# GpSimd's first zeroes moved ahead, the second weight block and four loads moved behind the first bias, eight zero groups for nine

## The chip, the cores and the metric

The kernel runs on one core of one Trainium2 chip. The metric is the device time of one execution in microseconds (us). Engines: TensorE (PE; its weight loads are PEld), VectorE (DVE), ScalarE (ACT), GpSimd (POOL), and SyncE (SP), whose queue issues most DMA transfers; ACT's queue issues a few.

## The reference

Attention over 4 batches of 8 heads (576 positions, 64 wide) with a causal mask and a forgetting bias, then two feed-forward layers on the 2304 x 512 result:

```python
scores = scale * np.matmul(q, k.transpose(0, 1, 3, 2))
cum = np.cumsum(np.maximum(s, 0.0), axis=-1)
bias = -(cum[:, :, :, None] - cum[:, :, None, :])
scores = np.where(causal, -1000000000.0, scores + np.minimum(bias, 0.0))
attn = softmax(scores)                    # with 1e-9 added to the sum
x = (attn @ v), heads side by side        # 2304 x 512
h = x @ w_in                              # 512 -> 2048
g = np.where(h >= 1, h, np.where(h <= -1, 0.0, (h + 1) ** 2 / 4))
x = g @ w_out                             # 2048 -> 512
out = ((x @ w_a) * (x @ w_b)) @ w_out2    # 512 -> 1536 -> 512
```

The weights arrive as 64-bit floats and are turned into 32-bit ones on the chip.

## The kernel before

The program is written as a list of some thousands of operations, each with the engine it runs on, an estimate of its time, a key (an intended moment) and the tiles that it reads and writes. A planner (`Plan.run`) walks through them on a simulated clock and takes on each engine the ready operation with the lowest key. So the order of the instructions on every engine comes from the keys, the estimates (`lat` for a transfer, the number in braces for an engine) and the earliest moments (`at`) in the code. A changed estimate can reorder instructions far from the place where it stands.

How work is staged: for each head, PE multiplies q by k for five blocks of up to 116 query rows (L731 for the first eight heads, which carry the bias as four more rows of q and k; L740 later, in split precision), DVE masks each block and takes its least value (L759, called "least"), ACT takes the exponential (L774), PE transposes it with an identity (L801), ACT or DVE copies the transposed block out (L397, L399), and for a pair of heads PE multiplies by v (L831). L865 spreads the inverse sums of a pair of heads for the first batch. In between the 64-bit weights are converted block by block: `wlow` and `wabs` on ACT (L978, L980), then four operations on DVE (`wclamp` L982, `wshift` L984, `wsign` L986, `wadd` L988), a cast to the high half on ACT or GpSimd (`whi`, L397 or L401) and the low half on DVE (`wlo`, L1004). From about 95 us on the two feed-forward layers run (L1034, L1245).

The first 15 us, which the change touches: PE multiplies zeros in groups of four 128x512 matmuls (L582, `WARM` groups). Tile `gate` takes the four parts of s and, in its second half, their running sum (`cums`, L650 to L657, on DVE). GpSimd builds `ones` (L587, L589), the mask `hide` (L632, L633), the identity, and zeroes part of the two `qk_tiles` (L601), which serve the split heads from the ninth head on. The bias rows of a head are DMAs out of `gate` into the head's raw tile `qkraw` (or `ysf`, for the third and fourth head), the ones rows are DMAs out of `ones`; both must land before the head's first score matmul. Two weight blocks fit in the staging tile `cvf`.

The function `fill`, called where the planner sees PE idle for over 0.5 us, issues matmuls on the zero tile `still` (L1471) if the idle stretch starts after a given moment of the planner's clock (`if lo < 8: return`). DMA queues run in order: an issue that waits holds up those behind it on the same engine.

Of the kernel before, what the change touches and what calls it, by code (L numbers as in the profile page):

```python
# [58 lines left out]
PAIRS = 2  # L59
WARM = 9  # L60
FILL = 0.5
# [253 lines left out]
def tile_forgetting_attention_two_ffn(  # L315
# [246 lines left out]
    for t in range(NG):  # L562
        dma(
            START + 2,
            lambda t=t: gate.t[t * BH : (t + 1) * BH, 0],
            lambda: s,
            BH * S * 4,
            (),
            [(gate, ("s", t))],
            "s",  # L570
            q=(SP, ACT)[t % 2],
        )
    s_parts = [(gate, ("s", t)) for t in range(NG)]
# [24 lines left out]

    op({POOL: 2.5}, START + 2, build_ones, (), [(ones, 0)], name="ones")
    for n in range(2):  # L600
        op({POOL: 1.6}, START + 6 + n, lambda e, n=n: nc.gpsimd.memset(f32(qk_tiles[n][:D, 2:4]), 0.0), (),  # L601
           [("q_zero", n)], name="zero")
# [62 lines left out]
    op({DVE: 0.4}, START + 2, cums(0), (), [(gate, "cum")], name="cum0")  # L665
    op({DVE: 3.9}, START + 3, cums(1), s_parts, [(gate, "cum")], name="cum1")
    op({ACT: 0.7}, later + 4, cums(2), [(gate, "cum")], ["terms0"], name="terms0", at=later - 5.0)
# [8 lines left out]
    def load_head(b, h, key):  # L676
# [5 lines left out]
        if b * H + h < QK32:  # L682
            st["qk"] = raw
            for w in range(2):
                dma(key, lambda w=w: raw.t[:D, w], lambda w=w: qk[bh, :, w], D * S * 4, (), [(raw, (0, w))], "qk", issue=0.6,
                    at=0.0 if bh < 2 else 8.4)
            first = bh == 0
            dma(START + 3 if first else key, lambda: raw.t[D : D + NG, 1], lambda: gate.t[:, 1].rearrange("(t h) n -> h t n", h=BH)[bh],
                NG * S * 4, [(gate, "cum")], [(raw, "bias")], "bias", issue=0.56)
            load_v(b, h, st, key)  # L690
# [21 lines left out]
    def load_v(b, h, st, key):  # L712
        vr = st["v"] = Ref(v_room, key)
        dma(key + 0.5, lambda: vr.t, lambda: v[b * H + h], P * NQ * D * 4, (), [(vr, 0)], "v", at=8.4)

# [233 lines left out]
    def convert(name, f, key):  # L949
# [3 lines left out]
        if paired:  # L953
            src = w[:, 2 * P * f : 2 * P * (f + 1)].rearrange("(c p) f -> p c f", p=P)
            soon = name == "in" and f == 0
            dma(START + 2.3 + 0.1 * f if soon else key - LEAD, lambda: wide.t.rearrange("p (c n) -> p c n", c=NC), lambda: src, P * 4096, (),
                [(wide, 0)], "wide", q=ACT if soon else SP, lat=WIDE_LAT)
        else:
# [504 lines left out]
    def fill(lo, hi, o, places):  # L1463
        taken = {n for r, where, _ in places if r.room is banks for n in where}
        if lo < 8:
            return
# [50 lines left out]
```

## Time and profile before

| | |
|---|---|
| device time, three runs | 1034.84, 1040.04, 1040.10 us; median 1040.04 |
| the profiled execution: device time | 1048.49 us |
| its span, first to last instruction | 1046.8 us |
| TensorE's granted clock, mean over the span | 0.986 of full |
| busy: PE, DVE, ACT, GpSimd | 98%, 79%, 56%, 9% |

The profiled execution took 8.45 us more than the median of the runs, and 1.69 us of its time lie outside the span. A granted clock of 1.00 is the upper of TensorE's two levels (2.4 GHz), 0.50 the lower (1.2 GHz). Busy shares are means over the whole span; the first 60 us and the rest have different limits.

### The profile page before, as it was taken

To read this page: it belongs to the slowest core of one execution; us is meant where nothing else is said; L and a number is where in the kernel's file an instruction comes from. 1 tells how busy PE (TensorE), PEld (TensorE's weight loads), DVE (VectorE), ACT (ScalarE), POOL (GpSimd) and SP (SyncE) were. 2 spreads that over 40 slices of the span, in tenths; PEclk is the share of its full clock that TensorE was granted. 3 is DMA by queue.
4 is the path that set the end of the run, shared out by engine and by line. 5 is a ranking of instruction groups with operands and counts; after the bars stand their busy time and mean duration, and the time that the engine had idled before them with its cause. 6 is when DMAs were issued, how large, how long until landed. Compare 5 with 4: busy or idle time off the path is not lost.

```text
span 1046.8 us, 18557 instructions
## 1 busy us (share of the span) xinstructions
PE 1029.4 (98%) x6829; PEld 960.8 (92%) x6829; DVE 824.5 (79%) x1594; ACT 584.7 (56%) x1233; POOL 93.0 (9%) x125
## 2 busy tenths in 40 slices
PE   8999999999999999999999999999999999999998
PEld 4668879998888999999999999999999999999998
DVE  6699988549899999997989798586984658872765
ACT  4688887568578775576474754443443324433330
POOL 2133222103222110000000000000000000000000
PEclk7799999999999999999999999999999999999999
DMA  7476678847767679568273575546554433472501
GB/s 206 133 205 196 199 215 278 251 161 245 238 222 241 205 261 313 201 223 266 81 267 106 170 254 195 184 170 229 210 202 153 171 131 134 173 256 92 182 1 61
DMA packets 89916, 201.00 MB, mean 192 GB/s; under 512 B 9697, under 2 KB 40673, under 8 KB 89057
## 3 DMA queue, kind: packets, MB, share of 16 engines
q1 hardware_dynamic: 89168, 199.11, 57.0%
q8 instruction: 54, 0.88, 0.3%
q10 hardware_dynamic: 656, 0.71, 0.2%
q14 instruction: 38, 0.30, 0.1%
HBM read 146.96 MB, written 52.22 MB: 190 GB/s over the span
## 4 chain that ended last, share of the span: by engine, by line
PE 77%; DVE 12%; ACT 4%; DMA 3%; issue 3%; POOL 1%; SPq 0%; DVEq 0%; POOLq 0%; ACTq 0%
PE pp L1034 29%; PE pp L1245 18%; PE ps L1245 13%; PE ps L1034 5%; PE ps L831 4%; PE ps L801 3%; PE ps L740 2%; DVE p L759 1%; PE ps L731 1%; DMA cvf<-in_w_in 1%; DVE ysf L1343 1%; PE pp L740 1%; DVE cvf L986 1%; DVE cvf L988 1%; DVE g L1080 1%
## 5 line engine op out<-in xcount | busy, mean ns | idle before, releaser
L1034 PE MATMUL pp<-g,whl 128*128 128x288 f32 (+1 forms) x1920 | 296.0, 309 | 2.3 <-DVE xcf L1277 1.1
L1034 PEld LDWEIGHTS pp<-g,whl 128*128 128x128 f32 x1920 | 281.9, 188 | 5.9 <-DVE xcf L1277 1.6
L1245 PE MATMUL pp<-form,xbt 128*128 128x384 f32 (+1 forms) x480 | 88.3, 321 | 0.4 <-DVE xbt L1134 0.4
L774 ACT ACTIVATE p<-p,mx 116x464 f32<-116x464 f32 (+4 forms) x140 | 81.8, 587 | 10.8 <-DVE mx L759 10.3
L1245 PE MATMUL pp<-form,xat 128*128 128x384 f32 (+1 forms) x480 | 87.6, 321 | 0.0
L1034 PE MATMUL ps<-g,whl 128*128 128x384 f32 (+1 forms) x480 | 81.0, 317 | 0.0
L1245 PEld LDWEIGHTS pp<-form,xbt 128*128 128x128 f32 x480 | 77.5, 188 | 1.1 <-DVE xbt L1134 0.6
L1245 PEld LDWEIGHTS pp<-form,xat 128*128 128x128 f32 x480 | 77.3, 188 | 0.9 <-DVE esf L1264 0.9
L1343 DVE TENSOR_TENSOR ysf<-pp,ysf 128x576 f32<-128x576 f32 (+1 forms) x62 | 51.1, 826 | 32.8 <-PE pp L1034 32.7
L1034 PEld LDWEIGHTS ps<-g,whl 128*128 128x128 f32 x480 | 75.9, 188 | 0.1
L397 ACT COPY pt<-ps 112x112 f32<-112x112 f32 (+4 forms) x175 | 64.7, 398 | 12.9 <-PE ps L801 12.1
L1245 PE MATMUL ps<-form,xbt 128*128 128x384 f32 (+1 forms) x360 | 66.3, 320 | 0.0
L1245 PE MATMUL ps<-form,xat 128*128 128x384 f32 (+1 forms) x360 | 65.8, 321 | 0.0
L801 PE MATMUL ps<-ident,p 116*116 116x116 f32 (+2 forms) x420 | 63.9, 271 | 1.7 <-ACT pt L397 0.7
L759 DVE CUSTOM_DVE_ANT_0 p<-ps,hide 116x116 f32<-116x116 f32 (+1 forms) x112 | 49.0, 451 | 18.8 <-PE ps L740 11.9
L978 ACT ACTIVATE cvf<-cvf 128x512 uint32<-128x512 uint32 x68 | 46.3, 680 | 26.8 <-DVE cvf L988 21.5
L1245 PE MATMUL pp<-form,cvt 128*128 128x384 f32 x288 | 58.0, 338 | 0.9 <-DVE form L1211 0.4
L1245 PEld LDWEIGHTS ps<-form,xbt 128*128 128x128 f32 x360 | 58.3, 188 | 0.2 <-DVE esf L1264 0.2
L1245 PEld LDWEIGHTS ps<-form,xat 128*128 128x128 f32 x360 | 58.0, 188 | 0.1
L801 PEld LDWEIGHTS ps<-ident,p 116*116 116x116 f32 (+2 forms) x420 | 46.8, 138 | 12.3 <-ACT pt L397 4.0
L831 PE MATMUL ps<-pt,v 116*64 116x344 f32 (+4 forms) x448 | 56.0, 391 | 0.0
L1129 DVE TENSOR_TENSOR sums<-sums 128x256 f32<-128x256 f32 x128 | 54.2, 424 | 2.1
(165 smaller groups left out, 1923.4 us busy)
## 6 DMA issues: line engine op xcount, KB each, us to landing
whl<-keep_out SPq DMA_DIRECT2D x60, 512.0 KB
qkraw<-in_qk SPq DMA_DIRECT2D x104, 144.0 KB
cvf<-in_w_out SPq DMA_DIRECT2D x28, 512.0 KB
keep_out<-whl SPq DMA_DIRECT2D x28, 512.0 KB
sums<-keep_b SPq DMA_DIRECT2D x36, 256.0 KB
keep_in<-whl SPq DMA_DIRECT2D x16, 512.0 KB
cvf<-in_w_in SPq DMA_DIRECT2D x15, 512.0 KB
cvf<-in_w_a SPq DMA_DIRECT2D x12, 512.0 KB
```

Source lines behind the costliest of these rows:

```text
L397: nc.scalar.copy(o, i)
L731: nc.tensor.matmul(pv()[:r, a, :w], t.t[: D + NG, 0, QT * i : n], t.t[: D + NG, 1, a * w : (a + 1) * w], start=True, stop=True,)
L740: nc.tensor.matmul(pv()[:r, a, :w], t.t[:, 2 * u, QT * i : n], t.t[:, 2 * u + 1, a * w : (a + 1) * w], start=(u == 0), stop=(u == 1),)
L759: nc.vector.tensor_tensor_reduce(out=psl(pref.t)[:r].rearrange("q (g n) -> q g n", g=parts), in0=pv()[:r, :parts, :w], in1=hide[:r, lag : ...
L774: nc.scalar.activation(p, p, AF.Exp, bias=mx.t[:r], scale=-1.0, accum_out=sm.t[:r, h % 2, i : i + 1])
L801: nc.tensor.transpose(pt.t[: rows[j], (j - j0) * QT : (j - j0) * QT + r], psl(pref.t)[:r, QT * j : QT * j + rows[j]], ident[:r, :r],)
L831: nc.tensor.matmul(ps.t[n * D : (n + 1) * D, q0 - lo : hi - lo], st["v"].t[: rows[j], j], st["pt"][g].t[: rows[j], REG_AT[g][j] + q0 - lo ...
L978: op({ACT: act(512) + 0.07}, k, lambda e: nc.scalar.activation(up(), low(), AF.Copy, scale=2.0**-29), [(wide, 0)], [(we, 0)], name="wlow")
L1034: nc.tensor.matmul(bank_of(ps, a)[:, :w1], w(wu), x(xu)[:, a * w1 : (a + 1) * w1], start=(k == 0 and t == 0), stop=(k == len(terms) - 1 an ...
L1129: return lambda e: nc.vector.tensor_tensor(one(o), one(x), one(y), op=how)
L1245: nc.tensor.matmul(at(to), by_pair(st.t)[:, at_w, wu, g], forms[b, layer, g].t[:, x, xu], start=fresh and k == 0, stop=k == len(terms) - 1 ...
L1343: nc.vector.tensor_tensor(o, i, o, op=ALU.add)
```

## The change

It moves GpSimd's two zeroings of `qk_tiles` ahead of `ones` (keys START+1, with an estimate of 1.0 for 1.6), issues one zero group less, lets `fill` act only from 14 us of the planner's clock, gives the second weight block an earliest moment of 9.5, v one of 9.0 for 8.4 and the q and k of the third and later heads 9.6 for 8.4, and changes four estimates (s transfers 2.6 for 2.0, the first bias transfer 1.2 for 2.0, `cums` 3.4 for 3.9, `ones` 2.2 for 2.5).

```diff
-WARM = 9
+WARM = 8
...
             q=(SP, ACT)[t % 2],
+            lat=2.6,
...
-    op({POOL: 2.5}, START + 2, build_ones, (), [(ones, 0)], name="ones")
+    op({POOL: 2.2}, START + 2, build_ones, (), [(ones, 0)], name="ones")
     for n in range(2):
-        op({POOL: 1.6}, START + 6 + n, lambda e, n=n: nc.gpsimd.memset(f32(qk_tiles[n][:D, 2:4]), 0.0), (),
+        op({POOL: 1.0}, START + 1 + 0.1 * n, lambda e, n=n: nc.gpsimd.memset(f32(qk_tiles[n][:D, 2:4]), 0.0), (),
            [("q_zero", n)], name="zero")
...
-    op({DVE: 3.9}, START + 3, cums(1), s_parts, [(gate, "cum")], name="cum1")
+    op({DVE: 3.4}, START + 3, cums(1), s_parts, [(gate, "cum")], name="cum1")
...
-                    at=0.0 if bh < 2 else 8.4)
+                    at=0.0 if bh < 2 else 9.6)
...
-                NG * S * 4, [(gate, "cum")], [(raw, "bias")], "bias", issue=0.56)
+                NG * S * 4, [(gate, "cum")], [(raw, "bias")], "bias", issue=0.56, lat=1.2 if first else 2.0)
...
-        dma(key + 0.5, lambda: vr.t, lambda: v[b * H + h], P * NQ * D * 4, (), [(vr, 0)], "v", at=8.4)
+        dma(key + 0.5, lambda: vr.t, lambda: v[b * H + h], P * NQ * D * 4, (), [(vr, 0)], "v", at=9.0)
...
-                [(wide, 0)], "wide", q=ACT if soon else SP, lat=WIDE_LAT)
+                [(wide, 0)], "wide", q=ACT if soon else SP, lat=WIDE_LAT,
+                at=9.5 if name == "in" and f else 0.0)
...
-        if lo < 8:
+        if lo < 14:
             return
```

On SP's queue at the start of the program (`cvf<-in_w_in` is a weight block, `qkraw<-in_qk` q and k of a head, `qkraw<-g` its bias, `ysf` the third and fourth head). Before:

```order
L409 DMA qkraw_75<-in_qk 64x576 x2
L409 DMA cvf<-in_w_in 128x4x256
L409 DMA qkraw_74<-g_199 4x576
L409 DMA v_282<-in_v 128x320
L409 DMA qkraw_75<-g_199 4x576
...
L409 DMA ysf<-g_199 4x576
L409 DMA cvf<-in_w_in 128x4x256
L409 DMA qkraw_74<-in_qk 64x576 x2
```

and of the change, the same place:

```order
L409 DMA qkraw_75<-in_qk 64x576 x2
L409 DMA qkraw_74<-g_200 4x576
L409 DMA v_281<-in_v 128x320
L409 DMA qkraw_75<-g_200 4x576
...
L409 DMA ysf<-g_200 4x576
L409 DMA qkraw_74<-in_qk 64x576 x2
L409 DMA qkraw_74<-g_200 4x576
L409 DMA cvf<-in_w_in 128x4x256 x2
```

The first bias now stands directly behind the first two heads' q and k; the second weight block moved from ahead of it to behind the fifth head's q, k and bias, where it goes out together with the third.

On DVE, from the last operation of the running sum to the second "least" of the first head. Before:

```order
L657 TENSOR_SCALAR g_199<-g_199,mids 128x576
L982 TENSOR_SCALAR cvf<-cvf 128x512
...
L988 ISA cvf<-cvf 128x1024
L982 TENSOR_SCALAR cvf<-cvf 128x512
L984 TENSOR_SCALAR cvf<-cvf 128x512
L759 ISA p_0_299,mx_0_300<-ps_82,hide 116x116
L759 ISA mx_0_300 116x1
L759 ISA p_0_309,mx_0_310<-ps_83,hide 116x232
```

and of the change (lines from L573 on stand one to two further down):

```order
L658 TENSOR_SCALAR g_200<-g_200,mids_72 128x576
L984 TENSOR_SCALAR cvf_211<-cvf_211 128x512
...
L990 ISA cvf_211<-cvf_211 128x1024
L1006 TENSOR_TENSOR whl0_285<-cvf_211,whl0_285 128x2x256
L760 ISA p0_0_290,mx0_0_291<-ps0_82,hide_70 116x116
L760 ISA mx0_0_291 116x1
L760 ISA p1_0_294,mx1_0_295<-ps1_83,hide_70 116x232
```

Two operations on the second weight block no longer stand ahead of the first "least"; the low half of the first block stands there in their place. Its high half is cast on ACT now, which GpSimd did before.

On GpSimd, the start of the program. Before:

```order
L587 MEMSET g_202 4x576
L589 ISA
L589 AFFINE_SELECT g_202<-g_202 4x576 x2
...
L601 MEMSET qk_77 64x1152
L601 MEMSET qk_78 64x1152
L912 MEMSET sm_268 116x10
```

and of the change:

```order
L602 MEMSET qk_77 64x1152
L602 MEMSET qk_78 64x1152
L588 MEMSET g_217 4x576
L590 ISA
L590 AFFINE_SELECT g_217<-g_217 4x576 x2
L633 MEMSET hide 116x580
```

The two zeroings moved from the end of GpSimd's first stretch to its beginning; the instructions themselves are the same.

## Rows read from the trace of the kernel before

**Rows 1.** The page: span; PE's granted clock in 40 slices, tenths.

```profile
span 1046.8 us, 18557 instructions
...
PEclk7799999999999999999999999999999999999999
```

**Rows 2.** Windows, PE: start:end, length, busy (x), clock, DMA share, GB/s.

```profile
11.29:12.76 1.47, 0.01 (x2) 1.00 0.84 260
12.76:14.17 1.41, 1.40 (x6) 1.00 0.72 217
14.17:14.61 0.44, 0.00 (x0) 0.56 0.49 75
14.61:37.70 23.09, 23.09 (x77) 0.50 0.50 155
37.70:41.50 3.80, 3.80 (x15) 0.50 0.08 33
```

**Rows 3.** Timeline of DVE, 0 to 15 us: start, length, instruction.

```profile
4.25 2.28 DVE L652 TENSOR_SCALAR g<-g 128x576 f32<-128x576 f32 x1 [2.30 <-DMA g<-in_s]
...
8.60 0.52 DVE L657 TENSOR_SCALAR g<-g,mids 128x576 f32<-128x576 f32 x1
9.10 0.43 DVE L982 TENSOR_SCALAR cvf<-cvf 128x512 f32<-128x512 f32 x1
...
10.74 0.69 DVE L988 CUSTOM_DVE_ANT_0 cvf<-cvf 128x1024 uint16<-128x1024 uint16 x1
13.48 0.43 DVE L982 TENSOR_SCALAR cvf<-cvf 128x512 f32<-128x512 f32 x1 [2.04 <-ACT cvf L980]
...
14.28 0.27 DVE L759 CUSTOM_DVE_ANT_0 p<-ps,hide 116x116 f32<-116x116 f32 x1
```

**Rows 4.** Timeline of GpSimd, 0 to 7 us.

```profile
4.16 2.05 POOL L601 MEMSET qk<- 64x1152 f32 x2
```

**Rows 5.** Timeline of ACT and of its queue (ACTq), 0 to 15 us.

```profile
2.86 2.07 ACTq L409 DMA_DIRECT2D qkraw<-g  x2
4.96 1.28 ACT L978 ACT_TABLE_LOAD   x1 [4.96 <-issue]
7.83 0.67 ACT L978 ACTIVATE cvf<-cvf 128x512 uint32<-128x512 uint32 x1 [1.59 <-DMA cvf<-in_w_in]
```

**Rows 6.** Timeline of SP's queue, 0 to 15 us.

```profile
8.07 0.41 SPq L409 DMA_DIRECT2D cvf<-in_w_in  x1
9.15 0.62 SPq L409 DMA_DIRECT2D qkraw<-g  x1
```

**Rows 7.** Chain that ended last, 0 to 16 us: start, length, what.

```profile
8.07 4.68 DMA cvf<-in_w_in
...
14.61 1.89 PE ps L731 x2
```

**Rows 8.** Windows: PE, PEld, DVE, ACT, GpSimd busy, clock, DMA share, GB/s.

```profile
14.61:41.50 26.89, 26.89 (x89) 17.66 (x91) 15.90 (x46) 13.49 (x40) 2.06 (x4) 0.50 0.44 138
...
42.10:57.30 15.20, 15.08 (x99) 10.50 (x98) 14.05 (x40) 12.83 (x38) 3.33 (x5) 1.00 0.68 215
...
42.10:95.50 53.40, 52.02 (x359) 38.42 (x358) 50.29 (x138) 45.82 (x131) 16.91 (x22) 1.00 0.69 210
```

**Rows 9.** Groups by line, DVE, 42.1 to 96 us: busy us, mean ns.

```profile
L399 DVE COPY pt<-ps 116x232 f32<-116x232 f32 (+5 forms) x11 | 4.5, 415 | 0.9 <-ACT g L774 0.5 <-PE ps L801 0.2
L988 DVE CUSTOM_DVE_ANT_0 cvf<-cvf 128x1024 uint16<-128x1024 uint16 x6 | 4.1, 686 | 0.0
L1004 DVE TENSOR_TENSOR whl<-cvf,whl 128x512 fp32r<-128x512 f32 x6 | 4.1, 682 | 0.0
```

**Rows 10.** Tile whl on ACT: ns least/median/most, first and last start.

```profile
L397 ACT CAST whl<-cvf x13: 608/622/627, 153.2 to 579.4; 128x512 fp32r<-128x512 f32 x13
```

**Rows 11.** Timeline of PE: the zero groups, and the first pair's product with v.

```profile
1.26 9.27 PE L582 MATMUL ps<-esf 128*128 128x512 bf16 x36 [1.26 <-DVE esf L576]
...
37.69 4.42 PE L831 MATMUL ps<-pt,v 116*64 116x344 f32 x20
```

## Prediction

> **What bounds the kernel now.** I read the page first. The span is 1046.8 us, and the granted clock stands at its upper level in every slice but the first two [rows 1]. So only the first 50 us look unlike the rest. I then cut them into windows of PE: after the zero matmuls and the filler PE idles 1.47 us, runs the first six score matmuls in 1.41 us, idles 0.44 us, and in that second pause the clock falls to its lower level [rows 2]. It stays there from 14.61 to 41.50 us with PE busy all the time. It comes back inside the first pair's twenty matmuls with v, which begin at 37.69 [rows 2, 11]. In this stretch DVE is busy 15.90 of 26.89 us and ACT 13.49 [rows 8]: PE at the lower clock sets the pace. From 42 us to the first feed-forward step, about 95 us, DVE is busy 50.29 of 53.40 us beside a PE at 52.02 [rows 8]; both are near their limit there.
>
> Last I read the chain of waits up to 15 us. It runs through the second weight block (4.68 us from issue to landing), ACT's and DVE's work on that block, the first "least" (L759), and from 14.61 on the second batch of score matmuls, which needs the bank that "least" empties [rows 7]. DVE's timeline shows why: its queue is in order, its work on the first block ends at 11.43 (10.74 + 0.69), then it waits for the second block, and the first "least" starts only at 14.28 [rows 3].
>
> **The change part by part.** *Second weight block behind the bias.* It takes two DVE operations out from ahead of the first "least", and the wait for the block with them. What stands there now is the low half of the first block, which waits for the high half, now on ACT. Worked out: DVE ends the first block at 11.43 as before [rows 3]; the cast on ACT takes 0.62 us by the row of later casts there [rows 10], so 12.05, with the hand-overs about 12.1; the low half takes 0.68 [rows 9], so 12.8. "Least" starts at 12.8 to 12.9 for 14.28: 1.4 us earlier.
>
> Is anything else late then? The bias must have landed. SP issued it at 9.15, behind the block [rows 6]; PE could start at 12.76 [rows 2], at most 3.6 us after the issue. With no block ahead it lands no later than that. Even at 12.76 the first of the three score blocks is through by about 13.1, and the gain is 1.2. Lower bound of the gain on this path 1.0, upper 1.4; I take 1.3, since both ends lie close.
>
> *Zeroes first.* VectorE's first operation on s took 2.28 us at 4.25, while one on the same tile with the same shape took 0.52 [rows 3]; the zeroing ran on GpSimd from 4.16 to 6.21 [rows 4], and the slow operation ended 0.3 us behind it. Moved, the zeroes run from about 0.8 on, when DVE waits for s anyway. At 4.25 GpSimd is then still at `ones` or the mask, in shorter instructions. So the stall shrinks by 0 to 1.76 us. This brings the running sum and the bias forward, but "least" hangs on the weight block (12.8), not on the bias, so I cost it at nothing. If that cover went, at most 1.76 us would show. `ones` is ready 2.05 us later, near 4.9 for 2.86. ACT issues its two transfers then. Before, the two took 2.07 us and the table load 1.28 [rows 5]; so ACT is free between 7.4 (two plain issues of some 0.6 each) and 8.3, and it needed the weights only at 7.83 [rows 5]. That costs 0 to 0.45 us, and is the 1.0 above.
>
> *One zero group less, and no filler.* Both run while PE has nothing else to do; they free no time. The zeroes end a microsecond sooner, near 9.5 (1.26 + 9.27 x 32/36) [rows 11], and no filler follows. If the bias lands between 10 and 11.5, PE again has a pause before the six score matmuls and a second one, 11.4 to 12.9 or so, behind them. Before, pauses of 1.47 and 0.44 us were followed by the lower clock [rows 2]; pauses at least as long should bring it too. The order has the same work up to the first pair's matmuls with v, so I carry over 23.09 + 3.80 us at the lower clock unchanged, begun 1.3 us earlier.
>
> *Blocks converted later.* By the order, between the first pair's scaling (42 us) and the first feed-forward step DVE gets three more copies of transposed blocks, two more low halves and one addition less than before: 3 x 0.415 + 2 x 0.682 - 0.686 = 1.9 us [rows 9]. Idle DVE time there is 3.11 us [rows 8]. So this costs between nothing, if it goes into those gaps, and 1.9 us; I take 0.5, nearer to nothing, since ACT has fewer copies in return. The later estimates and moments (v, q and k of later heads, transfers of s) only change when the planner wants them; SP's order shows v behind its head's bias as before, and I cost them at nothing: v is first read behind all of a pair's scores. From about a fifth of PE's order on, the two programs have the same sequence; what PE gains before is kept to the end.
>
> Sum: -1.3 + 0.5 = -0.8 us on a profiled execution of 1048.49 us, so 1047.7. That execution is 8.45 us above the median of the three runs; on the median, 1040.04 - 0.8 = **1039.2 us**. With the bounds the terms alone reach from -1.8 (nothing lost on DVE, and the 1.4, with some of the stall) to +0.9 (1.0 gained, 1.9 lost): 1038 to 1041. The clock makes the wide range. Three runs of one program lie 5 us apart, and the profiled one 8 above them; the stretch at the lower clock is the one place that I see which could differ so much between executions.
>
> **Rivals.** *The clock stays up, or returns early.* Against it stands that less PE work covers the first 13 us than before, and that 26.89 us of full PE work did not lift it [rows 8]. For it speaks that PE goes from zeroes to scores with a shorter first pause if the bias lands by 10, and that a run at 1034.84 exists. Price: the stretch of 26.89 us would be bound by DVE's 15.90 [rows 8], 11 us less; the second pair of heads, at the upper clock, took 15.20 [rows 8], which agrees. 1039.2 - 10 = 1029; if it returns half-way, 1034.
>
> The Trainium skill's page TensorE: Matmul & The Clock Gate (Part 1) says that the lower rate is the idle state and that sustained activity releases it. By that rule the clock should return soon after 14.61, since PE is never idle, and the time would be near the 1034 of the half-way case or below it. The trace disagrees: 0.50 for 26.89 us at a PE shown busy throughout [rows 8]. I go by the rows.
>
> *The clock returns one pair later: slower.* The place is the first pair's matmuls with v. The clock rose 3.8 us after their start, with 0.6 us of them left [rows 2, 11]. If it does not rise within them, the next such run of twenty is a pair later, and that pair's 15.20 us [rows 8] become about as long as the first pair's 27.5 (14.61 to 42.10): +12, so 1051. It decides between the cases whether those twenty matmuls are just long enough; that the work begins 1.3 us earlier could tip it.
>
> *DVE or weights late.* The third to fifth weight blocks stand two to nine places later on SP's queue. If one is late for its feed-forward step, PE waits a conversion (five DVE operations, some 3 us): 1042; two such, 1045.
>
> *Nothing comes of it.* ACT's cast, now ahead of the first "least", comes 1.4 us late, behind ACT's own transfers: 1040, no change.
>
> **Chances.** Half a per cent, 5.2 us, is about what a measurement tells from no change: below 1034.8 is faster, above 1045.2 slower. My forecast with the small rivals (DVE, weights, nothing) has 0.57, all of it within that. The clock up or early: 0.27, nearly all faster. A pair later: 0.11; weights late twice or more: 0.05; both slower. So faster 0.27, same 0.57, slower 0.16. For 8 in 10 the range takes in all of the middle, the clock up at 1029, and the late weights; part of the pair-later case stays out: 1029 to 1047. The likeliest case alone: 1037 to 1042.
>
> **What would show it.** Right: DVE's first operation on s well under 2.28 us; the second weight block issued after 15 us; the first "least" at 12.8 to 13.3; the clock at its lower level from about 13 to 40 us, rising in the first pair's matmuls with v; those starting near 36.4; the same PE order and idle time from 160 us on. Wrong: a clock that stays at the upper level through 15 to 40 us, or is still at the lower one at 45; or PE waiting for weights between 60 and 160 us by more than the trace of before shows.

## The result: the change is half a per cent slower

| | before | changed |
|---|---|---|
| median of 20 executions | 1039.13 us | 1045.22 us |
| least and most | 1034.73, 1051.27 | 1037.14, 1051.39 |
| the profiled execution, its span | 1048.49, 1046.8 | 1050.23, 1048.4 |
| mean granted clock of the profiled execution | 0.986 | 0.988 |

The ratio of changed to before is 1.0056, with a 95% interval from 1.0032 to 1.008. The forecast was 1039.2 us and no change that can be told; the time lies inside the stated range of 1029 to 1047 and 6 us above the forecast.

The twenty times of the changed kernel fall into groups by their mean granted clock: 7 executions at 0.999 or 1.0 took 1037.14 to 1040.12 us (median 1039.17), 4 at 0.993 took 1042.89 to 1045.54, and 9 at 0.988 to 0.991 took 1045.75 to 1051.39. Of the kernel before, 148 executions with a listed clock lie beside the experiments below, e1's twelve among them (two more, and one each of e14 and e16, took 1090 us and more; they were disturbed and are left out of every count): 54 at 0.999 or more (median 1035.72), 74 at 0.996 to 0.998 (median 1039.18), and only 20 at 0.993 or less (median 1048.9). So both profiled executions, before and changed, are of the low-clock kind. That kind is 13 of 20 for the changed kernel and 20 of 148 for the one before.

The page of the changed kernel, span and PE's clock in 40 slices; it answers to [rows 1] and looks nearly as before:

```profile
span 1048.4 us, 18534 instructions
...
PEclk8799999999999999999999999999999999999999
```

Windows of PE, answering to [rows 2] and [rows 8] (start:end, length, busy, clock, DMA share, GB/s):

```profile
10.60:12.04 1.44, 1.41 (x6) 1.00 0.32 76
12.04:14.40 2.36, 0.00 (x2) 1.00 0.74 215
14.40:16.00 1.60, 1.60 (x6) 0.97 0.69 213
16.00:38.00 22.00, 22.00 (x79) 0.50 0.35 100
38.00:40.00 2.00, 2.00 (x10) 0.55 0.79 253
40.00:42.00 2.00, 2.00 (x17) 1.00 0.29 81
```

The first six score matmuls now run at 10.6 us, and behind them PE stands still for 2.36 us in one piece. Before there were two pauses, 1.47 and 0.44 us, with those six matmuls between them. The clock falls near 15.9 and is back near 39.9: 24.0 us of a fully busy PE at the lower level, for 27 before.

The timeline of the changed kernel, all engines, 0 to 15 us, answering to [rows 3] to [rows 6] and [rows 11]:

```profile
0.80 2.04 POOL L602 MEMSET qk<- 64x1152 f32 x2 [0.29 <-POOLq L1512]
1.26 9.24 PE L583 MATMUL ps<-esf 128*128 128x512 bf16 x32 [1.26 <-DVE esf L577]
...
4.06 0.46 DVE L653 TENSOR_SCALAR g<-g 128x576 f32<-128x576 f32 x1 [2.11 <-DMA g<-in_s]
...
5.07 1.82 ACTq L409 DMA_DIRECT2D qkraw<-g  x2
...
7.49 0.62 SPq L409 DMA_DIRECT2D qkraw<-g  x1
...
9.16 0.68 ACT L980 ACTIVATE cvf<-cvf 128x512 uint32<-128x512 uint32 x1 [0.96 <-DMA cvf<-in_w_in]
...
12.08 0.69 DVE L990 CUSTOM_DVE_ANT_0 cvf<-cvf 128x1024 uint16<-128x1024 uint16 x1
...
12.81 0.62 ACT L397 CAST whl<-cvf 128x512 fp32r<-128x512 f32 x1 [2.41 <-DVE cvf L990]
...
13.46 0.69 DVE L1006 TENSOR_TENSOR whl<-cvf,whl 128x512 fp32r<-128x512 f32 x1 [0.68 <-ACT whl L397]
14.06 0.27 DVE L760 CUSTOM_DVE_ANT_0 p<-ps,hide 116x116 f32<-116x116 f32 x1
...
14.40 1.03 PE L732 MATMUL ps<-qkraw 68*116 68x464 f32 x2 [2.36 <-DVE mx L760]
```

The reader is to see three things. VectorE's first operation on s takes 0.46 us for 2.28, and the first bias leaves SP at 7.49 for 9.15: the front of the change works. The first weight block reaches ACT at 9.16 for 7.83, although its issue did not move; the table load was through at 8.2 (6.92 + 1.28), so it is the transfer that came late. And DVE stands at 12.77 with "least" next in need but the low half next in order: the low half waits 0.68 us for ACT's cast, runs 0.69, and "least" comes at 14.06, 0.22 us earlier than before.

The chain of the changed kernel up to 15 us, answering to [rows 7]:

```profile
1.74 7.40 DMA cvf<-in_w_in
...
12.81 0.62 ACT whl L397
13.43 0.03 issue
13.46 0.04 DVE whl L1006
13.49 0.57 issue
14.06 0.27 DVE p L760
...
14.40 1.03 PE ps L732 x2
```

It now runs through the first block for the second, and then through the cast and the low half.

Where did the time between the two profiled executions go? PE of the changed one is about 2 us ahead at 40 to 90 us, has lost that by 320 us, and loses another 1.7 us near 611 us, where ACT waits 2.4 us for transfers whose eight issues took SP's queue 4.96 us for 3.64 in the same order. That last is a chance of the execution: in e3's profile, of the same order, ACT waits 0.7 us there. The pair therefore doesn't explain the 6 us of the medians. The count of low-clock executions does, and it needed many executions to be seen: the changed kernel's seven high ones have a median of 1039.17 us, next to the 1039.13 of before's twenty.

One gain is hidden in this. None of the changed kernel's 20 executions lies at 0.996 to 0.998, where half of those of before lie (74 of 148). That group comes from a stall near 64 us, shown under e1 and e13, and the order of the change doesn't have it (e3, below).

### The profile page after: what moved, and what is told of

Same layout as the page of the kernel before. It is cut to its first block, busy times and chain, and to the rows that moved or that the text cites. A ratio compares the mean times of both kernels' runs of the same rounds, so it can differ in the third digit from the quotient of the medians.

```text
span 1048.4 us, 18534 instructions
## 1 busy us (share of the span) xinstructions
PE 1027.3 (98%) x6818; PEld 959.3 (91%) x6818; DVE 822.9 (78%) x1597; ACT 588.6 (56%) x1237; POOL 87.3 (8%) x118
## 4 chain that ended last, share of the span: by engine, by line
PE 75%; DVE 14%; DMA 3%; ACT 3%; issue 3%; POOL 1%; SPq 1%; ACTq 0%; DVEq 0%; POOLq 0%
PE pp L1036 28%; PE pp L1247 18%; PE ps L1247 13%; PE ps L1036 5%; PE ps L832 4%; PE ps L802 2%; DVE p L760 2%; PE ps L741 1%; PE ps L732 1%; DVE cvf L988 1%; DVE cvf L990 1%; DVE qk L708 1%; DVE g L1082 1%; DMA qkraw<-in_qk 1%; DVE whl L1006 1%
## 5 line engine op out<-in xcount | busy, mean ns | idle before, releaser
L397 ACT COPY pt<-ps 116x348 f32<-116x348 f32 (+5 forms) x172 | 63.0, 393 | 12.3 <-PE ps L802 11.6
L980 ACT ACTIVATE cvf<-cvf 128x512 uint32<-128x512 uint32 x68 | 46.2, 679 | 30.2 <-DVE cvf L990 24.9
L802 PEld LDWEIGHTS ps<-ident,p 116*116 116x116 f32 (+2 forms) x420 | 47.0, 138 | 13.2 <-ACT pt L397 4.0
```

Source lines behind the costliest of these rows:

```text
L397: nc.scalar.copy(o, i)
L802: nc.tensor.transpose(pt.t[: rows[j], (j - j0) * QT : (j - j0) * QT + r], psl(pref.t)[:r, QT * j : QT * j + rows[j]], ident[:r, :r],)
L980: op({ACT: act(512) + 0.07}, k, lambda e: nc.scalar.activation(up(), low(), AF.Copy, scale=2.0**-29), [(wide, 0)], [(we, 0)], name="wlow")
```

## The experiments

Each kernel was timed beside the one before on the same chip, in four groups (e1 to e4, e5 to e8, e9 to e12, e13 to e16), each on a chip of its own; ratios are against the kernel before of the same group. Its low share was 7 of 35, 2 of 35, 3 of 33 and 8 of 33 in these groups, so small differences in count mean little, and medians of different groups are compared only roughly. The median is that of all executions; "high" counts executions with a mean clock of 0.999 or more and gives their median, "low" those at 0.993 or less.

| run | median us | ratio, 95% interval | high | low | of |
|---|---|---|---|---|---|
| e1, before again | 1038.75 | 0.9987 (0.9957 to 1.0016) | 2, 1036.07 | 0 | 12 |
| e2, before, fewer zeroes | 1041.24 | 0.9997 (0.9955 to 1.004) | 3, 1035.29 | 5 | 12 |
| e3, changed, pause filled | 1037.62 | 0.9961 (0.9924 to 0.9997) | 12, 1037.62 | 0 | 12 |
| e4, before, pauses filled | 1038.19 | 0.9973 (0.9941 to 1.0006) | 5, 1035.92 | 0 | 12 |
| e5, changed, longer zeroes | 1038.86 | 1.0021 (0.9988 to 1.0054) | 7, 1037.83 | 4 | 12 |
| e6, changed without zeroes first | 1038.35 | 1.0009 (0.9985 to 1.0033) | 9, 1038.17 | 3 | 12 |
| e7, before, block late | 1040.70 | 1.0034 (1.0012 to 1.0057) | 7, 1039.88 | 1 | 12 |
| e8, changed without block late | 1046.61 | 1.0079 (1.0047 to 1.0112) | 5, 1040.48 | 6 | 12 |
| e9, changed, two neighbours swapped | 1038.20 | 1.0013 (0.9991 to 1.0036) | 8, 1037.76 | 3 | 12 |
| e10, changed, zeroes moved back | 1044.52 | 1.0047 (1.0013 to 1.0082) | 5, 1037.19 | 7 | 12 |
| e11, e4 with more filler | 1037.67 | 0.9998 (0.9987 to 1.001) | 11, 1037.67 | 0 | 11 |
| e12, changed, table load early | 1045.90 | 1.006 (1.0026 to 1.0095) | 4, 1038.24 | 5 | 9 |
| e13, e4 with one block earlier | 1035.64 | 0.9972 (0.9948 to 0.9995) | 11, 1035.57 | 0 | 12 |
| e14, before, zeroes first alone | 1039.92 | 1.002 (0.9992 to 1.0048) | 6, 1038.76 | 3 | 11 |
| e15, before, estimates alone | 1042.93 | 1.0038 (1.0 to 1.0075) | 5, 1040.15 | 3 | 12 |
| e16, before, eight groups alone | 1038.41 | 0.9979 (0.9949 to 1.0009) | 6, 1035.09 | 4 | 11 |

Two theories stood at the start: that the change loses the clock in the opening, by the pause behind the first six scores, and that its re-planned order makes PE wait later on. The rivals on the first were that less zero work alone loses it, and that something ahead of the low half comes late (the zeroings in one piece, or the table load). The expectations name them by letters.

The zeroes and the filler never reach the output; the other edits change only the order or the moments of work that is there anyway, but for e12's, whose small result is overwritten.

**e1, the kernel before once more.** No edit.

> The kernel before, unchanged, for the granted clock of each of its executions. Theory A (opening clock: the change makes TensorE's clock fall to its lower level more often or for longer in the first 40 us): most executions here show a mean granted clock of 0.995 or more, against 7 of 20 of the changed kernel; those at 1.00 take 1035 to 1037 us and the few at 0.988 take 1048 or more. Theory B (schedule: the re-planned order costs some us between 42 and 200 us whatever the clock does): the clocks are spread as in the changed kernel, and at equal clock this kernel is 3 to 6 us faster.

Measured: no execution with a low opening, and a profile of the common kind, at 1039.31 us. Its windows of PE:

```profile
16.00:38.00 22.00, 21.91 (x143) 1.00 0.80 241
...
63.00:66.00 3.00, 0.69 (x5) 1.00 1.04 227
66.00:68.00 2.00, 2.00 (x17) 0.81 0.94 380
68.00:70.00 2.00, 2.00 (x13) 0.50 0.10 39
```

The stretch from 16 to 38 us that ran at 0.50 in [rows 8] runs at 1.00. In the opening, the pauses of [rows 2] are missing too: PE runs its first eight score matmuls on end, though the second block still stands ahead of "least" on DVE.

```profile
12.03 2.39 PE L731 MATMUL ps<-qkraw 68*116 68x116 f32 x8
```

In place of the low opening a short dip follows a stall of PE near 64 us. The waits of PE from 58 to 68 us name ACT, and the waits of ACT the fifth block of the first feed-forward weight (`PE ps L801 <- ACT pt L397` and `ACT cvf L980 <- DMA cvf<-in_w_in`, 2.3 and 2.4 us, once each); the chain that ended last says the same:

```profile
57.35 7.42 DMA cvf<-in_w_in
...
64.85 0.18 ACT cvf L980
...
65.41 0.26 ACT pt L397
...
65.71 0.41 PE ps L801 x2
```

So the profiled execution of before was not the typical one.

**e2, fewer zeroes in the order of before.** The ninth group issues nothing, the filler acts from 14 us; no other instruction moves.

```diff
-               nc.tensor.matmul(idle.t, warm[:, :P], warm, start=True, stop=True) for _ in range(4)
...
+               nc.tensor.matmul(idle.t, warm[:, :P], warm, start=True, stop=True) for _ in range(4 if n < 8 else 0)
...
-        if lo < 8:
+        if lo < 14:
```

> The kernel before with only the four matmuls of the last zero group and the seven filler matmuls near 10 us left out; every other instruction and its order as before. Theory A: the longer pause ahead of the first scores (some 3.2 us for 1.5) brings the lower clock oftener: median 1042 to 1047, half of the executions at a mean clock under 0.994. Theory B: 1038 to 1040, as before.

Measured: a median 2.5 us above e1's, just under the 1042 to 1047 that theory A expected, and 5 of 12 executions at the low clock, for 7 of 35 of the kernel before in the same group. The ratio can't be told from 1. In its profile PE pauses 1.93 us ahead of the scores and the clock is low from about 13.2 to 30.2 us. Less zero work alone may make the low opening more common; twelve executions don't show it.

**e3, the changed kernel with its pause filled.** 22 matmuls on zeros behind the third score block of the first head.

```diff
+            if b == 0 and h == 0 and i == 2:
+                for _ in range(22):
+                    nc.tensor.matmul(banks.tiles[-1][:, : 2 * P], still[:, :P], still, start=True, stop=True)
```

> The changed kernel with 22 more matmuls on zeroes (2.4 us) issued behind the third score block of the first head, where PE paused 2.36 us; their result is not used, and the order is otherwise the same. Theory A: the clock holds at its upper level in nearly all executions, the mean clock is 0.998 or more, and the time falls to 1036 to 1039, at or under the kernel before. Theory B: the time falls by less, and stays 3 us or more above the kernel before with its own pauses filled.

Measured: all 12 executions at the high clock, 1036.86 to 1038.97 us, 7.6 us below the changed kernel's median. In its profile, the matmuls in the pause, then windows of PE: the stretch that was low, the one near 64 us, and a later one:

```profile
10.73 2.57 PE L750 MATMUL ps<-still 128*128 128x256 bf16 x22
```

```profile
16.00:38.00 22.00, 21.22 (x138) 1.00 0.71 214
...
63.00:66.00 3.00, 3.00 (x23) 1.00 0.95 242
...
72.00:160.00 88.00, 84.18 (x651) 1.00 0.80 239
```

and the later stretch in that of e1, the kernel before:

```profile
72.00:160.00 88.00, 86.42 (x660) 1.00 0.74 214
```

The pause is what makes the low clock frequent in the changed kernel: with it filled and nothing else touched, none of 12 executions is low, for 13 of 20. From 63 to 66 us PE never stands still, so the stall of e1 isn't there. The last line is another matter. At an equal clock PE idles 3.8 us there (88.00 - 84.18), and 1.6 in the kernel before.

**e4, the same for the kernel before.** Thirteen filler matmuls more ahead of the scores, four behind the third block.

```diff
-        for _ in range(min(20, int(0.8 * (hi - lo) / 0.108))):
+        for _ in range(min(20, int(0.8 * (hi - lo) / 0.108)) + (13 if lo < 14 else 0)):
```

> The kernel before with its two pauses filled: 13 more filler matmuls ahead of the first scores and 4 behind the third score block; the order is otherwise the same. Both theories: the clock holds in nearly all executions and the time is 1034 to 1037. Theory A says that the changed kernel with its pause filled lies within 2 us of this one, theory B that it lies 3 us or more above.

Measured: 1038.19, above the 1034 to 1037 that both theories expected; no execution at 0.993 or less, 5 at full clock (median 1035.92) and 7 at 0.998 (1037.5 to 1039.7). What is left between them is the dip near 66 us. So the fair comparison at full clock is 1035.7 to 1035.9 for the order of before and 1037.6 for that of the change.

**e5, the changed kernel with longer zeroes.** Its last group issues 11 matmuls for 4, the order unchanged.

```diff
+               nc.tensor.matmul(idle.t, warm[:, :P], warm, start=True, stop=True) for _ in range(4 if n < 7 else 11)
```

> The changed kernel with seven more zero matmuls at the end of the last zero group: the time that the ninth group and the filler took before, in one piece; order otherwise that of the changed kernel. Theory C (the pause behind the first scores, while the first least waits for the weight block, drops the clock): the zeroes now end near 12.3 us, the scores follow and the pause shrinks to some 0.5 us, so the clock holds in most executions, mean clock 0.997 or more, median 1037 to 1039. Theory D (the number of zero matmuls does not matter, the re-planned order keeps the clock low): a third or more of the executions still at 0.993 or less, median 1042 or more.

Measured: 7 executions at full clock, 4 low. In its profile the zeroes end at 12.2 and the scores follow without a pause. The median is as theory C expected, the third of low executions is what theory D named. Zero work ahead of the scores holds the clock less surely than e3. That the block's landing decides how much is needed would fit, but wasn't tried.

**e6, the change without its GpSimd part.** The two zeroings stay behind the mask; the planner then puts "least" ahead of the low half.

```diff
-    op({POOL: 2.2}, START + 2, build_ones, (), [(ones, 0)], name="ones")
+    op({POOL: 2.5}, START + 2, build_ones, (), [(ones, 0)], name="ones")
...
-        op({POOL: 1.0}, START + 1 + 0.1 * n, lambda e, n=n: nc.gpsimd.memset(f32(qk_tiles[n][:D, 2:4]), 0.0), (),
+        op({POOL: 1.6}, START + 6 + n, lambda e, n=n: nc.gpsimd.memset(f32(qk_tiles[n][:D, 2:4]), 0.0), (),
```

> The change without its GpSimd part: the tiles of the split heads are zeroed last again, ones first; eight groups and the rest as in the change. The order puts the first least ahead of the low half of the first block here. Theory C: the first least comes up to 0.7 us earlier, but the first operation on s stalls 1.8 us again in part of the executions and the scores come later; the pauses sum up to about the same, so clocks are spread as in the change (a third or more at 0.993 or less) and the median is 1040 to 1046. If zeroing first were what brought the lower clock (ones late, the table load late, so the weights' work late), the clock would hold in most executions, median 1037 to 1039.

Measured: 1038.35 us and 9 of 12 at full clock, which theory C did not expect and its rival, the zeroes first, did. That eight groups without filler lose the clock whatever else stands there falls with it. "Least" starts at 11.81 in its profile, and the eight score matmuls run on end (from 11.21, 2.22 us). But e6 moves the zeroings and swaps the low half and "least" at once; e9 and e10 take the two apart.

**e7 and e8, the second block's moment alone and left out.** e7 is the kernel before with the first line, e8 the changed kernel with the second.

```diff
+                at=9.5 if name == "in" and f else 0.0)
...
-                at=9.5 if name == "in" and f else 0.0)
```

> The kernel before with one part of the change: the second weight block gets its earliest moment of 9.5, so it moves behind the first bias; nine groups and the filler stay. Theory C: little pause in the opening as the zeroes reach 11.3 and the scores follow; clock 0.996 or more in most. Theory E (the moved block re-plans 40 to 200 us for the worse): executions at a full clock take 1037 to 1039, some 2 us more than those of the kernel before (1035.5). If the move is harmless they take 1034 to 1036.

> The change without that part: the second block is issued ahead of the first bias as before; eight groups and no filler. Theory C: the bias lands behind the block near 12 us, PE pauses some 1.5 to 2.5 us ahead of the scores, and the clock is low in a third or more of the executions; median 1041 to 1046. Theory E: its executions at a full clock take 1035 to 1036, as before.

Measured: with the block late alone, one execution of 12 at the low clock, but 1039.88 at full clock, some 4 us over before and above what theory E expected. Without it, 6 of 12 low and 1046.61 in all; at full clock it takes 1040.48, not the 1035 to 1036 of theory E. Its profile has a pause of 2.32 us ahead of the scores, since the bias is behind the block again and the zeroes are fewer:

```profile
12.40 2.19 PE L732 MATMUL ps<-qkraw 68*116 68x116 f32 x8 [2.32 <-DMA qkraw<-g]
```

So the late block isn't what costs the clock, and leaving it out doesn't cure the change. That profile is of an execution at full clock (1.000): a pause as long as the changed kernel's isn't followed by the lower clock every time.

**e9, two neighbours on DVE swapped.** The low half of the first block is made to stand behind the first "least"; nothing else in the program's order moves.

```diff
-           [(wr, 0), (hl, 0)], [(hl, 1)], name="wlo", port=True)
+           [(wr, 0), (hl, 0)] + ([(heads[0, 0]["mx"][0], 0)] if name == "in" and f == 0 else []), [(hl, 1)], name="wlo", port=True)
```

> The changed kernel with one pair of neighbours on DVE swapped: the low half of the first weight block behind the first least, not ahead of it; nothing else differs in the order of any engine. Theory F (the low half and its wait for ACT's cast, 1.3 us on DVE ahead of the first least, make the pause that drops the clock): the first least comes near 12.8, PE's pause behind the first scores shrinks from 2.4 to about 1.1 us, the mean clock is 0.998 or more in two thirds of the executions, median 1037.5 to 1040. Theory G (GpSimd's zeroing makes ones late, so ACT's transfers, table load and weight work come late): a smaller gain, a third or more still at 0.993 or less, median 1040 to 1046.

Measured: 1038.20 us, 8 of 12 at full clock (one more at 0.998), 3 low. The timeline of its profile, 10 to 13.5 us:

```profile
10.81 2.25 PE L732 MATMUL ps<-qkraw 68*116 68x116 f32 x8
11.09 0.69 DVE L990 CUSTOM_DVE_ANT_0 cvf<-cvf 128x1024 uint16<-128x1024 uint16 x1
11.70 0.27 DVE L760 CUSTOM_DVE_ANT_0 p<-ps,hide 116x116 f32<-116x116 f32 x1
11.81 0.62 ACT L397 CAST whl<-cvf 128x512 fp32r<-128x512 f32 x1 [2.41 <-DVE cvf L990]
...
12.46 0.69 DVE L1006 TENSOR_TENSOR whl<-cvf,whl 128x512 fp32r<-128x512 f32 x1 [0.49 <-ACT whl L397]
```

"Least" runs while ACT casts, the bank is free, and PE runs its eight score matmuls on end. One swap gives back 7 us of the median (1045.22 and 1038.20, of different groups) or 4.5 us by the ratios (1.0056 and 1.0013). The place of the low half is the part of the change's order that makes the pause. The count of low executions alone, 3 of 12 for 13 of 20, would be thin; with e6, e10 and e12 it is 6 of 24 where "least" stands ahead of the low half and 25 of 41 where it stands behind it (e8, which has "least" ahead, pauses for another reason, the late bias).

**e10 and e12, something late ahead of the low half?** e10 puts the zeroings behind the identity and leaves every other engine's order alone; e12 loads ACT's table at 2.22 us by a one-column activation behind the first block's issue.

```diff
-        op({POOL: 1.0}, START + 1 + 0.1 * n, lambda e, n=n: nc.gpsimd.memset(f32(qk_tiles[n][:D, 2:4]), 0.0), (),
+        op({POOL: 1.0}, START + 1 + 0.1 * n, lambda e: None, (),
...
+        make_identity(nc, ident)
+        for n in range(2):
+            nc.gpsimd.memset(f32(qk_tiles[n][:D, 2:4]), 0.0)
...
+                                                       nc.scalar.activation(mids, mids_in, AF.Abs)), (), [(wide, 0)], move=P * 4096,
...
```

> The changed kernel with the two zeroings on GpSimd put back behind the identity; no other engine's order differs from the change. Theory G: ACT's table load is back near 4.9 us, its work on the weights starts when the block lands, and the clock holds in two thirds or more of the executions: median 1037.5 to 1040. Theory F: the low half still stands ahead of the first least, so the pause stays in most executions, a third or more at 0.993 or less, median 1040 to 1046.

> The changed kernel with a one-column activation on ACT behind its third transfer, so that the table load comes ahead of the two transfers that wait for ones; no other order differs, but for one small zeroing on DVE near 1 us. Theory G: ACT's work on the weights starts as soon as the block has landed (6.6 to 9.1 us in the profiles so far) for 8.2 at the earliest, and the clock holds oftener, half or more of the executions at 0.999 or more, median 1038 to 1041. Theory F: as the change, median 1042 to 1047.

Measured: 1044.52 and 1045.90 us, 7 of 12 and 5 of 9 at the low clock, like the changed kernel and as theory F expected. Neither the place of the zeroings nor the table load is the cause. In e10's profile the stall on s is back (2.42 us), "least" starts at 13.93, and PE pauses 0.71 us ahead of the six scores and 1.47 behind them; the clock is low from about 16.2 to 29.8 us.

**e11 and e13, the dip near 64 us.** Both start from e4. e11 adds 20 matmuls on zeros behind the last score block of the eighth head. e13 issues the fifth block ahead of the eleventh head's q and k on SP.

```diff
+            if b == 0 and h == H - 1 and i == NQ - 1:
...
+                for _ in range(20 if spare else 0):
...
-                    [(raw, (u, w))], "qk", issue=0.6, lat=WIDE_LAT)
+                    [(raw, (u, w))], "put off" if bh == 10 else "qk", issue=0.6, lat=WIDE_LAT)
```

> The kernel before with its opening pauses filled as in the earlier run, and 20 matmuls on zeroes behind the last score block of the eighth head, near 63 us, where PE waited 2.3 us in two profiles and the clock fell for some 3 us after it. If that dip costs what its executions at 0.998 show beside those at 1.00 (1038.3 for 1035.5), the clock is 0.999 or more in nearly all and the median is 1035 to 1037, under both kernels. If the filler only takes PE's time, it stays at 1038 to 1040.

> The kernel before with its opening pauses filled, and on SP's queue one pair of neighbours swapped: the fifth w_in block ahead of the eleventh head's q and k, not behind them. Nothing else differs. In two profiles ACT waited 2.4 us for this block near 63 us and PE 2.3 us behind it, and the clock dipped. If the transfers ahead of the block make it late, the wait and the dip go: clock 0.999 or more in most executions, median 1035 to 1036.5. If the block is late because its slot in the staging tile comes free late, SP's queue is held up by it instead, q and k come late, and the median is 1038 to 1041.

Measured: e11 holds the clock in all 11 executions but takes 1037.67, above the 1035 to 1037 expected: its filler seems to cost about what the dip did. e13 takes 1035.64, as expected if the transfers ahead make the block late, with 11 of 12 at full clock for e4's 5, and beats the kernel before by 0.28% (ratio 0.9972, up to 0.9995). Windows of PE in e4 and then in e13:

```profile
63.00:66.00 3.00, 0.89 (x4) 1.00 1.05 224
66.00:68.00 2.00, 1.98 (x11) 0.54 0.99 399
```

```profile
63.00:66.00 3.00, 3.00 (x19) 1.00 1.08 223
66.00:68.00 2.00, 2.00 (x18) 1.00 1.06 263
```

The DMA engines are as full in both (1.05 and 1.08); the order of two issues decides here whether ACT, and behind it PE, stands still.

**e14, e15 and e16, the re-planned order taken apart.** At full clock the order of the change is 1.9 to 3.5 us slower than that of before (1037.62 in e3 and 1039.17 in the changed kernel, beside 1035.72). Each of these is the kernel before with one part of the diff: GpSimd's keys and estimates, the other three estimates, or `WARM` with the filler's moment.

```diff
+        op({POOL: 1.0}, START + 1 + 0.1 * n, lambda e, n=n: nc.gpsimd.memset(f32(qk_tiles[n][:D, 2:4]), 0.0), (),
...
+            lat=2.6,
...
+WARM = 8
```

> The kernel before with the GpSimd part alone (zeroes first, its two estimates). Its order puts the low half of the first block ahead of the first least, as the change does, while nine groups and the filler stay. Theory F: the low clock comes oftener than before (a fifth or more at 0.993 or less), median 1038 to 1042. Theory H (any re-planned order costs some 2 us at a full clock): executions at 0.999 or more take 1037 to 1039. Otherwise they take 1035 to 1036, as before.

> The kernel before with the changed estimates alone (s transfers, first bias, running sum). The first least stands ahead of the low half. Theory F: clocks as before (0.996 or more in four of five). Theory H: executions at 0.999 or more take 1037 to 1039; else 1035 to 1036.

> The kernel before with eight zero groups and no filler before 14 us alone, planned anew (the earlier run with fewer zeroes kept the order). The first least stands ahead of the low half; the pause ahead of the scores is as long as there. Theory F with the pause as the cause: clocks as in that run, a quarter at 0.993 or less, median 1039 to 1043. Theory H: executions at 0.999 or more take 1037 to 1039, against 1035.3 in that run with the old order.

Measured at full clock: 1038.76, 1040.15 and 1035.09 us, beside 1035.72 of before. That any new plan costs some 2 us falls with e16. It comes with the zeroes first, with the estimates and (e7) with the late block, each alone, and isn't the sum of them. The later moments of v and of q and k were not tried alone. What in those orders costs it isn't settled: the profile of e7, at full clock, idles 4.0 us from 72 to 160 us for e1's 1.6, but the profiles of e14 and e15 are not of full-clock executions (0.995 and 0.997) and can't be set beside it.

At the low clock were 3 of 11, 3 of 12 and 4 of 11, which can't be told from the 8 of 33 of before in this group; theory F's share for e14 is so neither shown nor refuted. Together with e7 it shows something else. Both have the low half ahead of "least" (e7's profile has it at 12.04 and 12.65), as the change has, but keep nine groups and the filler: 4 of 23 are low, for 25 of 41 with eight groups and no filler. So by these counts it takes both parts of the change, the swap on DVE and the thinner cover, to make the low clock the common case. The thinner cover without the swap has 6 of 24 (e6, e9) and 9 of 23 (e2, e16); whether that is more than before can't be told. Nor is the opening the only place for it: in e14's profile PE waits 1.6 us for a copy on ACT near 23 us, and the clock is low from there to about 34 us.

## Why the prediction was wrong

**What was right.** The stall on s (0.46 for 2.28), the bias 1.66 us earlier, the second block behind it on SP, the low half ahead of "least", a pause behind the six scores (one of 2.36 us, with none ahead of them), and in the profiled execution a low clock up to the first pair's product with v. That the profile shows these signs is luck: in 7 of 20 executions the clock stayed up, which the prediction names as a sign of being wrong. It is luck too that 1045.22 lies in the range, whose upper end was drawn for late weight blocks; PE's longest wait from 60 to 160 us is 0.5 us in the changed kernel's profile, for 1.0 before. The slower side was named, but with another mechanism: the clock did not return a pair later, it fell more often.

**The step that failed: "I carry over 23.09 + 3.80 us at the lower clock unchanged".** It took the opening of one execution as that of the kernel, on both sides of the change. The number that spoke against it stood in the text: the profiled execution took 8.45 us more than the median, and the low executions of before lie 9.7 us above its middle group (1048.9 and 1039.18). Had the stretch been taken as the exception, the question would have been whether the change makes it more common, and the pause that the prediction itself drew (11.4 to 12.9) would have been a loss of some 10 us in some share of executions: 13 of 20. Between the medians of the changed kernel's high and lowest groups lie 10.4 us (1039.17 and 1049.58). e3 shows that the pause is what makes the low clock frequent, e9 and e10 that the low half's place on DVE makes the pause, and e7 and e14 that it takes the thinner cover as well. For the same reason the gain of 1.3 us was added to the wrong base: in e1's profile, of the common kind, PE doesn't wait for the first "least" at all, so there the 1.3 us could not be saved.

**"They free no time."** True of zeroes and filler, but they are cover: with the low half ahead of "least", 4 of 23 executions are low with nine groups and filler and 25 of 41 with eight groups and none. They also ended at 10.5, not near 9.5. The prediction took all 36 as equally long, but the first ones stand 0.43 us apart and the later ones 0.21, and the same 32 matmuls took 9.24 us here, 8.36 in e3's profile and 9.72 in e9's.

**The first "least" at 12.8.** The term was 1.3 us, the pair of profiles shows 0.22. The working of the four operations and the cast held (1.98 us from the start of L990 to "least", for 2.1 forecast: 12.8 less 10.74); it started 1.34 us later, as the block landed later. In e12, with the same order on DVE, the block reached ACT at 7.39 and "least" ran at 12.29. A transfer's landing was given no range.

**"I take 0.5"** for the re-planned order: at full clock it is 1037.62 - 1035.72 = 1.9 us (e3's median less that of before), the upper end of its bounds. That they meet proves nothing: the term was for copies and low halves on DVE up to 95 us, and where the 1.9 us are lost is open.

**The rival "the clock stays up"**, priced at 1029, was in truth the common case of the kernel before (128 of 148) and 7 of 20 of the changed one, and its price was from the wrong base: 10 us below 1048.5, not below 1039.

**The rule on the clock.** The prediction has the clock come back inside the first pair's twenty matmuls with v. That was one execution: in the profiles of e2 and e10 it is back at about 30.2 and 29.8 us, before those matmuls begin (34.18 and 32.72). So the low stretch has no fixed length: some 17 and 14 us there, 24 in the changed kernel's profile and 27 in that of before. Over 16 to 38 us the changed kernel's PE is busy 22.00 of 22.00 at 0.50. The Trainium skill's page TensorE: Matmul & The Clock Gate (Part 1) has sustained activity release the lower rate; this trace disagrees again, with PE shown busy throughout as in [rows 8]. What made the clock come back, and why one execution in seven of the kernel before loses it, is not shown by any run. What keeps it up is shown: of the 47 executions of e3, e4, e11 and e13, whose pauses are filled, none was low.

## What to carry to other kernels

Compare the profiled execution's time with the median before reasoning from its clock; if they differ, take another profile, and count executions by clock, since a change can act on how often a state occurs and not on what it costs. On an in-order engine a wait that is taken away lets the planner put something else there that waits too: look at what stands directly ahead of the operation that frees the next engine, since one swap of two neighbours was worth 4 to 7 us here, and one of two transfers took 11 of 12 executions to full clock for 5 of 12 (e13 and e4). Work on zeros that seems to fill nothing may be cover for a clock: before thinning it, find the longest pause that is left. Two parts of a change that do little alone can do much together, so undo each of them from the whole and also try each alone.

## What the runs showed of the chip that was not expected

The same first weight block, issued at the same place, reached ACT between 6.59 us (e1) and 9.16 us (changed), at once on landing in both. The same zero matmuls need 8.36 to 9.72 us for 32, with the clock shown at 1.00 all the while; they start 0.43 us apart at first and 0.21 later, and the moment at which this changes differs between executions (near 3.8 us in e3's profile, 6.7 in e9's). A stall of 2.3 us near 64 us was followed by the lower clock within 3 us (0.81 and 0.50 in e1's windows), and a pause of 2.36 us at 12 us by 24 us of it; a pause of 0.55 us in e9's opening, and one of 2.32 us in e8's, was followed by none in its profile.
